# A kernel of attention and SwiGLU: the last unit's gated product taken in two parts, and seven groups of steps moved along the engine queues

## The chip, the cores and the metric

The kernel runs on one core of one Trainium2 chip. The metric is the device time of one execution in microseconds (us), as the median of several executions.

## The reference

Input `x` has 2048 rows of 576. Attention `a` has 32 heads of width 18 and four segments of 512 rows; it mixes softmax attention inside a segment with a memory `M`, `z` that earlier segments have filled. The feed-forward part `b` is a SwiGLU with an inner width of 4608. A sigmoid gate per row mixes the two.

```
g = sigmoid((x * gate_w).sum(-1))
q, k, v = x @ wq, x @ wk, x @ wv            # 32 heads of 18, segments s = 0..3 of 512 rows
per segment: p = softmax(q k^T * 18**-0.5 + mask);  a_dot = p @ v
             a_mem = phi(q) M / (phi(q) z + 1e-6);  o = sigmoid(beta) a_mem + (1 - sigmoid(beta)) a_dot
             M += phi(k)^T v;  z += sum phi(k)       # phi(t) = t + 1 if t > 0 else exp(t)
a = o @ wo
b = (silu(x @ w_gate) * (x @ w_up)) @ w_down     # 576 -> 4608 -> 576
out = g * a + (1 - g) * b
```

## The kernel before

TensorE (PE in the profile) works with operands split into a high and a low part, so that each product is made of several matmuls. The program has three stages, and each engine carries out its instructions in the order in which the code below issues them; no scheduler moves them.

**Stage 1, the segments.** The loop `for s in range(NSEG)` (L732) goes through four segments. In each come nine chains `qk(s, m, u, mid)` (n = 0 to 8, L735 to L781) of 14 matmuls (L223) into three banks in turn, for 128 columns of q or k each. ScalarE (ACT) and VectorE (DVE) split a finished chain into three bf16 parts (L455, L462, L465, and GpSimd, POOL, L466), and make phi of it (L460, L461, L468). The list `mid` holds steps of other kinds that are issued in the middle of that: `rest_sum` and `rest_split` (L651 to L658, x's last 64 rows for stage 2; tables `RSTEP` and `blocks`) in segment 2, and `first_sum` and `first_split` (L628 to L641, x for stage 2; tables `FSUM`, `FSPLIT`) in segment 3. After each chain from the second on, `next(upd)` takes one step of `upd_gen` (L496): it transposes a block of phi(k) into two banks, copies them to the tile `kt` (512 columns by ACT, L514; 64 columns by DVE, L517), and one step later multiplies it with v (L505). Then follow eight value steps `v_step` (L475: 14 matmuls L223, then ACT L484, L485, DVE L486, ACT L491, POOL L492) on the banks 5, 6 and 7 in turn, each with a memory step (`mem_step`, PE L550, DVE L553 to L557). In segment 3 these eight also issue the first steps of `w_make(0)`, which splits the first unit's weights (POOL L369, ACT L373, DVE L377, then a store): the tuple at L835 says how many per value step.

**Stage 2, the units.** Rows are taken in two halves of 1024, and the inner width in 36 tiles of 128 (f = 0 to 35): 72 units. A unit (L1510 to L1553) makes gate and up for one tile by seven products (`seven`, L1421: six matmuls L1426 and one L1429 each) into the banks `a`, `y` and `xx`, in this order: `a` 0, `y` 1, `a` 2, `xx` 3, `a` 4, `y` 5, `xx` 6. ACT copies `a` into `xx` after the first (L1519); product 2 adds into `a` and so has to wait for that copy. After 5 and 6 come the two Silu (L1540, L1542) and the two gated products on DVE (L1548 for rows 0 to 511, which needs product 6; L1549 for rows 512 to 1023, which doesn't). `split_by` has them split into `hh` (ACT L1295) and `hl` (DVE L1298). Behind each product but one stands a `tick()` (two behind 5), k = 0 to 7, which issues what `defer` put down for that beat, the down products of the last three units, and a step of attention.

The down products are 16 groups per three units, `feed(half, f)` in the order of i = 0 to 7 with two column parts each; i = 0 to 3 reads rows 0 to 511, i = 4 to 7 the others. `down_groups` (PE L1162, nine matmuls a group; the first two groups at once, so that each takes the two older tiles before the newest) adds into `ya` by DVE (L1169, L1171). Down weights are split by `d_split` (ACT L1139, DVE L1140, then L1142 or ACT L1144) under a scale from `d_look` (ACT L1116, a Square with a sum) and `d_scale` (PE L158, DVE, POOL L1128 to L1131). After unit 35 of each half the groups of the last three tiles are fed at once; in half 0 ten beats work them off (L1557), which also issue `rest_second` (POOL L1381, ACT L1388, DVE L1392), x's last rows for half 1.

`exp_table()` (L1418) has ACT load the table set for Exp ahead of its use; Silu needs another set. `gates()` (L1412) makes the row gates from an Exp.

**Stage 3** multiplies attention with `wo`, mixes and stores 16 row tiles.

Of the kernel before, what the change touches and what calls it, by code (L numbers as in the profile page):

```python
# [18 lines left out]
OP = mybir.AluOpType  # L19
# [9 lines left out]
FT = 36  # L29
# [40 lines left out]
def gated_mix(ctx, tc, xT, xrest, wf, wfr, wfh, wd, wv, wo, beta, cmask, ident, bmask, out):  # L70
# [323 lines left out]
    with ExitStack() as st:  # L394
# [101 lines left out]
        def upd_gen(s):  # L496
            acc = [pair_tile([P, 3, MW]), pair_tile([P, 2, MW])]
            Mo, Mn = Mm[s % 2], Mm[(s + 1) % 2]
            for i in range(5):
                if i:  # L500
                    for k in range(NT):
                        a, b = HR[k]
                        n = (b - a) * E
                        kk = P if k < 4 else 64
                        nc.tensor.matmul(acc[k // 3][:kk, k % 3, :n], kt[:, P * k:P * k + kk],  # L505
                                         vf[:, i - 1].rearrange("p h e -> p (h e)")[:, a * E:b * E],
                                         start=(i == 1 and k % 3 == 0), stop=(i == 4), skip_group_check=True)
                if i < 4:
                    kt = sp.tile([P, D], F32, name="kt", bufs=1)
                    c = slice(P * i, P * i + P)  # L510
                    ta = half_tile([P, 4, P])
                    for k in range(4):
                        nc.tensor.transpose(ta[:, k], phi[s, k, 1][:, c], idt)
                    nc.scalar.activation(kt[:, 0:512], ta.rearrange("p a b -> p (a b)"), AF.Copy)  # L514
                    tb = lone_tile([P, P])
                    nc.tensor.transpose(tb, phi[s, 4, 0][:, c], idt)
                    nc.vector.tensor_copy(kt[:, 512:576], tb[:, 64:128])  # L517
# [140 lines left out]
            rest_16(XR[j], rr[((0, 0), (0, 0), (1, 1), (0, 1), (1, 0), (1, 1), (0, 1))[j]])  # L658

        XR = [None] * 7  # L660
        RSTEP = {2: (0, 3), 3: (5, -1), 4: (1, -4), 5: (4, -2), 6: (2,), 7: (-6,), 8: (6,)}
        rb, rs = {}, {}

        def b_load(i):
# [56 lines left out]
        def scan_load(t):  # L721
# [7 lines left out]
        FSUM = {3: [(1, 0), (4, 0)], 4: [(2, 0), (1, 1)], 6: [(4, 1), (2, 1)], 7: [(6, 0)], 8: [(6, 1)]}  # L729
        FSPLIT = {2: [(0, 0)], 3: [(5, 0), (0, 1)], 4: [(1, 0), (4, 0)], 5: [(5, 1), (2, 0)], 6: [(1, 1), (3, 0)],  # L730
                  7: [(3, 1), (4, 1)], 8: [(2, 1)]}
        for s in range(NSEG):  # L732
            upd = upd_gen(s - 1) if s else None
            casts = []
            for n, (m, u) in enumerate(chains):  # L735
                mid = []
                if s == 0:
                    for z in loads.get(n, []):
                        z()
                    if n + 3 < 9:  # L740
                        mid.append(lambda n=n: q_split(*chains[n + 3]))
                    if n in halves:
                        mid.append(lambda n=n: v_split(*halves[n]))
                if s == 1 and n < 3:
                    cast = masks(*((0, 3), (3, NT), (0, 0))[n])
                    casts.append(cast)
                if s == 1 and 3 <= n < 6:
                    mid.append(casts[n - 3])
                if (s, n) == (1, 7):
                    mid.append(betas)  # L750
                mid += scan_step(17 * s + n)
                if (s, n) == (1, 7):
                    mid.append(lambda: total(sx, 0, 20))
                if s == 2:
                    if n == 5:
                        mid.append(lambda: weigh(1, half_tile([P, 9])))
                    if n == 0:
                        rest_load()
                    for z in blocks.get(n, ()):
                        mid.append(lambda z=z: b_step(*z))  # L760
                    for j in RSTEP.get(n, ()):
                        mid.append(lambda j=j: rest_split(j) if j >= 0 else rest_sum(-j))
                if s == 3:
                    if n < 4:
                        first_load(n)
                    for j, z in FSPLIT.get(n, []):
                        if j in (0, 3, 5):
                            mid.append(lambda j=j, z=z: first_split(j, z))
                    for j, z in FSUM.get(n, []):
                        mid.append(lambda j=j, z=z: first_sum(j, z))  # L770
                    for j, z in FSPLIT.get(n, []):
                        if j in (1, 2, 4):
                            mid.append(lambda j=j, z=z: first_split(j, z))
                if s < 3:
                    for kt in ((0, 1), (2, 3), (4,))[n - 6] if s == 0 and n > 5 else (n - 4,) if s and n > 3 else ():
                        raws["x", kt] = x_load(s + 1, kt)
                qk(s, m, u, mid)
                flush(2)
                scan_load(17 * s + n)
                if upd is not None and n > 0:  # L780
                    next(upd, None)  # L781
# [16 lines left out]
            for n in range(8):  # L798
# [23 lines left out]
                else:  # L822
                    if n == 4:
                        wraw_of[1] = [w_load(1, u) for u in range(2)]
                    if n < 2:
                        first_split(6, n)
                    for k, t, v in ((0, rhs[0][96:], 0.0), (1, kst[0], -1.0), (3, kst[1], -1.0), (4, rhs[1][96:], 0.0)):
                        if n == k:
                            nc.gpsimd.memset(t, v)
# [13 lines left out]
    with ExitStack() as st:  # L843
# [271 lines left out]
        def d_look(f):  # L1115
            nc.scalar.activation(junk, draw[f], AF.Square, accum_out=column(123 + f % CH))  # L1116
# [253 lines left out]
        def rest_second(rest):  # L1370
# [23 lines left out]
            todo = [(-1, load, 0), (0, high, 0), (0, high, 3), (1, low, 0), (1, low, 3), (4, load, 1), (11, high, 5),  # L1394
                    (11, total, 1), (12, low, 5), (12, high, 1), (13, total, 4), (13, low, 1), (14, total, 2),
                    (14, high, 4), (15, low, 4), (15, total, 6), (16, high, 2), (16, low, 2), (17, high, 6), (18, low, 6)]
            return [(o, lambda fn=fn, j=j: fn(j)) for o, fn, j in todo]

        def glance(i, k):
# [34 lines left out]
        for pos, (half, f) in enumerate(seq):  # L1434
# [49 lines left out]
            def tick():  # L1484
# [5 lines left out]
                if half == 0:  # L1490
                    g = {(0, 0): f + 2, (2, 2): f + 1, (2, 4): f + 2}.get((q, k), FT) if f > 1 else k if f == 0 and k < CH else FT
                    if g < FT:
                        draw[g] = d_load(g)
                    if (f == 2 and k < CH) or (f > 2 and q == 0 and 2 <= k < 2 + CH):
                        d_look(k if f == 2 else f + k - 2)
                    if (f, k) == (2, 3) or (f > 2 and (q, k) == (0, 5)):
                        d_scale(f // CH)
                    if (f, k) == (2, 7) or (f > 2 and (q, k) == (1, 3)):
                        d_back(f // CH)
                    if f == 2 and k > 4 or f > 2 and (q, k) in ((1, 1), (1, 7), (2, 5 + int(f < FT - 1))):  # L1500
                        g = k - 5 if f == 2 else f - 1 if k == 1 else f
# [15 lines left out]
            p5, sg0, sg1 = (row_tile() for _ in range(3))  # L1517
            seven(a, 0)
            nc.scalar.activation(xx, a, AF.Copy)  # L1519
# [20 lines left out]
            nc.scalar.activation(sg0, sg0, AF.Silu, scale=iw[f // 4])  # L1540
            seven(y, 5, False)
            nc.scalar.activation(sg1, y, AF.Silu, scale=iw[f // 4])  # L1542
# [5 lines left out]
            nc.vector.scalar_tensor_tensor(sg0, xx, hk[f // 4], sg0, op0=OP.mult, op1=OP.mult)  # L1548
            nc.vector.scalar_tensor_tensor(sg1, p5, hk[f // 4], sg1, op0=OP.mult, op1=OP.mult)  # L1549
# [116 lines left out]
```

## Time and profile before

| | |
|---|---|
| median of 3 executions | 1716.42 us (1714.65 to 1716.99) |
| the profiled execution | 1718.78 us, of which its span is 1717.1 us |
| PE busy | 1679.5 us, 98% of the span |
| DVE, ACT, POOL busy | 1353.8, 1076.6, 889.2 us |
| granted TensorE clock | 0.998 in the mean |

The span is the time from the first to the last instruction. Stage 1 ends at some 233 us of it, half 0 at 923 us, half 1 at 1631 us. In the answers of the trace, "[0.54 <-ACT bank L1519]" behind an instruction says that its engine was idle for 0.54 us before it and which instruction ended that wait; a row with "x6" merges six instructions.

### The profile page before, as it was taken

What the parts mean: (1) busy time and instruction counts of PE and PEld (TensorE: products, weight loads), DVE (VectorE), ACT (ScalarE), POOL (GpSimd) and SP (SyncE); (2) the same over time, 40 slices, a digit from 0 to 9 for tenths busy, and PEclk for the clock granted to TensorE, in tenths of its full rate; (3) what the DMA queues carried; (4) which work ended last, traced back from release to release, by engine and by line L of the source; (5) the groups of instructions that cost most, each with busy time, mean ns of one, the idle gap of its engine ahead of it and who ended that gap; (6) DMA issues with size and microseconds to landing.
All of it is one profiled execution on the core that took longest, in us unless ns stands there. A gap on an engine that the chain in (4) does not pass through costs nothing.

```text
span 1717.1 us, 35318 instructions
## 1 busy us (share of the span) xinstructions
PE 1679.5 (98%) x12269; PEld 1077.8 (63%) x12269; DVE 1353.8 (79%) x3295; ACT 1076.6 (63%) x1930; POOL 889.2 (52%) x1191
## 2 busy tenths in 40 slices
PE   9999999999999999999999999999999999999999
PEld 7898865556655665565555656556656656655577
DVE  6687676789888988898886878788878788776466
ACT  7666567777777777767774654665556566565411
POOL 3336562266667665665452665465546565554121
PEclk9999999999999999999999999999999999999999
DMA  8666675666776675446535486796696597574544
GB/s 282 218 232 222 214 260 208 208 200 177 231 223 208 168 244 192 154 121 195 169 123 164 114 192 158 163 219 136 147 215 166 121 221 167 140 163 125 156 157 145
DMA packets 349542, 314.25 MB, mean 183 GB/s; under 512 B 201268, under 2 KB 266548, under 8 KB 349364
## 3 DMA queue, kind: packets, MB, share of 16 engines
q1 hardware_dynamic: 349364, 312.00, 63.5%
q8 instruction: 96, 1.57, 0.4%
q14 instruction: 82, 0.67, 0.1%
HBM read 186.15 MB, written 99.55 MB: 166 GB/s over the span
## 4 chain that ended last, share of the span: by engine, by line
PE 73%; DVE 12%; ACT 7%; issue 3%; DMA 3%; POOL 1%; SPq 1%; DVEq 0%; ACTq 0%; POOLq 0%
PE bank L1426 31%; PE bank L1162 18%; PE bank L223 8%; PE bank L1429 5%; PE bank L889 3%; PE bank L1002 2%; DVE ya L1171 1%; PE bank L1030 1%; ACT L1540 1%; DVE junk L907 1%; PE bank L1032 1%; PE bank L964 1%; DVE p L1102 1%; ACT row L1540 1%; DMA rc<-rt 1%
## 5 line engine op out<-in xcount | busy, mean ns | idle before, releaser
L1162 PE MATMUL bank<-dw,hh 128*128 128x320 f16 (+1 forms) x2304 | 437.5, 286 | 13.3 <-DVE ya L1171 8.9
L1162 PE MATMUL bank<-dw,hl 128*128 128x320 f16 (+1 forms) x1152 | 330.1, 287 | 3.8 <-DVE hl L1298 3.2
L1106 POOL TENSOR_TENSOR p<-pe,p 128x512 f16<-128x512 f32 x220 | 271.9, 1236 | 75.3 <-DVE p L1102 50.6
L1162 PEld LDWEIGHTS <-hh 128*128 128x128 f16 x2304 | 225.3, 98 | 99.9 <-issue 18.1
L1006 ACT ACTIVATE pe<-bank 128x512 f32<-128x512 f32 x220 | 130.1, 592 | 183.6 <-PE bank L1002 167.5
L1171 DVE SCALAR_TENSOR_TENSOR ya<-bank,sc,ya 128x320 f32<-128x320 f32 x352 | 176.2, 511 | 55.0 <-PE bank L1162 53.3
L1429 PE MATMUL bank<-xr,rh 128*128 128x512 f16 x504 | 191.0, 379 | 0.0
L907 DVE CUSTOM_DVE_ANT_0 junk<-bank,cm 128x128 bf16<-128x128 f32 (+2 forms) x352 | 169.3, 481 | 13.7 <-PE bank L889 7.3
L1298 DVE SCALAR_TENSOR_TENSOR hl<-hh,row 128x512 f16<-128x512 f16 x144 | 129.7, 902 | 45.7 <-ACT hh L1295 44.8
L1014 POOL TENSOR_SCALAR_AFFINE_SELECT pe<-pe 128x256 f32<-128x256 f32 (+1 forms) x220 | 89.3, 406 | 144.9 <-ACT pe L1006 137.3
L1162 PEld LDWEIGHTS <-hl 128*128 128x128 f16 x1152 | 112.7, 98 | 34.3 <-DVE hl L1298 3.8
L889 PE MATMUL bank<-kst,qst 108*128 108x512 bf16 (+3 forms) x512 | 124.5, 299 | 3.6 <-ACT pe L1006 2.9
L1002 PE MATMUL bank<-qst,kst 111*128 111x512 bf16 (+3 forms) x352 | 103.2, 300 | 1.1 <-DVE acc L975 1.1
L1102 DVE CAST p<-pe 128x512 f16<-128x512 f32 x203 | 103.3, 510 | 0.0
L369 POOL TENSOR_TENSOR ws<-raw 128x256 f32<-128x256 f32 x72 | 65.6, 912 | 63.4 <-DMA raw<-in_wf_dram 32.2
L1538 DVE TENSOR_TENSOR row<-bank,row 128x512 f32<-128x512 f32 x72 | 49.6, 689 | 60.9 <-ACT bank L1537 60.8
L223 PE MATMUL bank<-xo,qhi 128*128 128x512 f32 x288 | 92.5, 401 | 1.3 <-ACT xo L132 0.7
L466 POOL TENSOR_TENSOR q<-qr,q 128x512 bf16<-128x512 f32 x36 | 47.8, 1329 | 84.8 <-ACT q L465 77.0
L1295 ACT ACTIVATE hh<-row 128x512 f16<-128x512 f32 x144 | 89.0, 618 | 3.7 <-DVE row L1548 3.0
L1533 ACT ACTIVATE row<-bank 128x512 f32<-128x512 f32 x72 | 42.9, 596 | 73.7 <-PE bank L1429 73.7
L1537 ACT ACTIVATE bank<-bank 128x512 f32<-128x512 f32 x72 | 41.9, 581 | 72.8 <-PE bank L1429 70.9
L1429 PEld LDWEIGHTS <-rh 128*128 128x128 f16 x504 | 49.3, 98 | 59.6 <-issue 0.2
(1102 smaller groups left out, 4213.9 us busy)
## 6 DMA issues: line engine op xcount, KB each, us to landing
xo<-in_wf_dram SPq DMA_DIRECT2D x65, 320.0 KB
raw<-in_wf_dram SPq DMA_DIRECT2D x72, 256.0 KB
dc<-dw SPq DMA_DIRECT2D x36, 432.0 KB
dw<-dc SPq DMA_DIRECT2D x36, 432.0 KB
rh<-rc SPq DMA_DIRECT2D x72, 168.0 KB
draw<-in_wd_dram SPq DMA_DIRECT2D x36, 288.0 KB
xo<-in_xT_dram SPq DMA_DIRECT2D x33, 256.0 KB
vd<-vps SPq DMA_DIRECT2D x8, 912.0 KB
```

Of the source, the lines that this page charges most:

```text
L223: nc.tensor.matmul(t, st[n], mv[n], start=(n == 0), stop=(n == 13))
L889: nc.tensor.matmul(t[:, c:c + w], qs[:KR, pr, P * i:P * i + P], ks[:KR, pr, 0:w], start=True, stop=True)
L907: nc.vector.tensor_tensor_reduce(junk.bitcast(BF)[:, :w], t[:, c:c + w], cm[:, L - w:L], 1.0, -3.0e38, OP.add, OP.max, m[:, k:k + 1])
L1002: nc.tensor.matmul(t[:, c:c + w], ks[:KR + 3, pr, P * j:P * j + P], qs[:KR + 3, pr, P * j:L], start=True, stop=True)
L1006: nc.scalar.activation(pe, t, AF.Exp, scale=SCALE)
L1102: nc.vector.tensor_copy(p1, pe)
L1106: nc.gpsimd.tensor_sub(p2, pe, p1)
L1162: nc.tensor.matmul(t, p, d[:, q, cs], start=(f == CH * c and n == 0), stop=(f == CH * c + CH - 1 and n == 2))
L1171: nc.vector.scalar_tensor_tensor(ya[:, i, cs], t, inv[c], ya[:, i, cs], op0=OP.mult, op1=OP.add)
L1298: nc.vector.scalar_tensor_tensor(lo, hi, -STEP, src, op0=OP.mult, op1=OP.add)
L1426: nc.tensor.matmul(t, w[:, p, z], x[z][:, q], start=first and n == 0, stop=False, skip_group_check=True)
L1429: nc.tensor.matmul(t, rem[:, RPOS[j]], XR[j], start=False, stop=True, skip_group_check=True)
```

## The change

Eight edits, all of order; no product is added or left out.

1. `kt`: its last 64 columns are copied by ACT instead of DVE.
2. Segment 2: `rest_sum(6)` goes from chain 7 to chain 6, and `rest_split(6)` from the middle of chain 8 to behind it.
3. Segment 3: `first_sum(6, 1)` and `first_split(2, 1)` go from chain 8 to the value steps 1 and 0; `first_split(6, z)` from value steps 0 and 1 to 2 and 3.
4. The first weights' steps are issued about one value step earlier.
5. `rest_second`: its second part two beats later.
6. The three first `d_look` go from unit 2 to unit 1, `d_scale` from beat 3 of unit 2 to beat 1; the last `d_split` of half 0 from beat 5 of unit 35 to beat 2.
7. No Exp table in unit 0 and at the start of unit 3; `gates()` at the end of unit 3.
8. In unit 35 the gated product of rows 512 to 1023 comes ahead of product 6, those rows are split first, and the 16 groups start with i = 4 to 7.

```diff
-                    nc.vector.tensor_copy(kt[:, 512:576], tb[:, 64:128])
+                    nc.scalar.activation(kt[:, 512:576], tb[:, 64:128], AF.Copy)
...
-        RSTEP = {2: (0, 3), 3: (5, -1), 4: (1, -4), 5: (4, -2), 6: (2,), 7: (-6,), 8: (6,)}
+        RSTEP = {2: (0, 3), 3: (5, -1), 4: (1, -4), 5: (4, -2), 6: (2, -6)}
...
                 qk(s, m, u, mid)
+                if (s, n) == (2, 8):
+                    rest_split(6)
...
-                    if n < 2:
-                        first_split(6, n)
+                    if n == 0:
+                        first_split(2, 1)
+                    if n == 1:
+                        first_sum(6, 1)
+                    if 2 <= n < 4:
+                        first_split(6, n - 2)
...
-                    for _ in range((0, 0, 2, 1, 2, 2, 2, 2)[n]):
+                    for _ in range((0, 1, 2, 2, 2, 2, 2, 2)[n]):
...
         def feed(half, f):
-            return [(f // CH, i, hf, hs, ds, half) for i in range(8) for hf in range(2)]
+            return [(f // CH, i, hf, hs, ds, half) for i in ((4, 5, 6, 7, 0, 1, 2, 3) if f == FT - 1 else range(8))
+                    for hf in range(2)]
...
-                    if (f == 2 and k < CH) or (f > 2 and q == 0 and 2 <= k < 2 + CH):
-                        d_look(k if f == 2 else f + k - 2)
-                    if (f, k) == (2, 3) or (f > 2 and (q, k) == (0, 5)):
+                    if (f == 1 and 4 <= k < 4 + CH) or (f > 2 and q == 0 and 2 <= k < 2 + CH):
+                        d_look(k - 4 if f == 1 else f + k - 2)
+                    if (f, k) == (2, 1) or (f > 2 and (q, k) == (0, 5)):
                         d_scale(f // CH)
...
-                    if f == 2 and k > 4 or f > 2 and (q, k) in ((1, 1), (1, 7), (2, 5 + int(f < FT - 1))):
+                    if f == 2 and k > 4 or f > 2 and (q, k) in ((1, 1), (1, 7), (2, 6 if f < FT - 1 else 2)):
...
-            if half == 0 and q == 0 and f:
+            if half == 0 and q == 0 and f > CH:
                 exp_table()
-                if f == CH:
-                    gates()
...
-            if (half or q == 0) and not cps:
+            if (half or q == 0 and f) and not cps:
                 exp_table()
+                if half == 0 and f == CH:
+                    gates()
             tick()
             tick()
+            gated = [lambda: nc.vector.scalar_tensor_tensor(sg0, xx, hk[f // 4], sg0, op0=OP.mult, op1=OP.mult),
+                     lambda: nc.vector.scalar_tensor_tensor(sg1, p5, hk[f // 4], sg1, op0=OP.mult, op1=OP.mult)]
+            parts, first = [(hh[:, z], hl[:, z], (sg0, sg1)[z]) for z in range(2)], int(f == FT - 1)
+            if first:
+                gated[1]()
             seven(xx, 6, False)
-            nc.vector.scalar_tensor_tensor(sg0, xx, hk[f // 4], sg0, op0=OP.mult, op1=OP.mult)
-            nc.vector.scalar_tensor_tensor(sg1, p5, hk[f // 4], sg1, op0=OP.mult, op1=OP.mult)
-            split_by(2, hh[:, 0], hl[:, 0], sg0, int(q < CH - 1))
-            split_by(3, hh[:, 1], hl[:, 1], sg1)
+            gated[0]()
+            if not first:
+                gated[1]()
+            split_by(2, *parts[first], int(q < CH - 1))
+            split_by(3, *parts[1 - first])
```

The tables `FSUM` and `FSPLIT` lose their entries of chain 8, and the second part of `rest_second`'s list has every beat raised by two.

**Place one**, DVE at the end of half 0 (unit 35): before, from the sum that follows product 4 (L1538) to the first addition into `ya`. L1140 and L1142 split the last down weight, L1355 belongs to half 1's x.

```order
L1538 TENSOR_TENSOR row<-bank_11775,row 128x512
L1355 SCALAR_TENSOR_TENSOR xo_10317<-xr_10334,sc,xo_10317 128x512
L1140 SCALAR_TENSOR_TENSOR dw<-draw,sc,dw 128x576
L1548 SCALAR_TENSOR_TENSOR row<-bank_11842,sc,row 128x512
L1549 SCALAR_TENSOR_TENSOR row<-row,sc 128x512
L1142 TENSOR_SCALAR dw<-dw 128x576
L1298 SCALAR_TENSOR_TENSOR hl<-hh,row 128x512 x2
```

The same place with the change; L1146 and L1148 are the down weight, L1543 the sum, L1555 and L1554 the gated products, L1304 `hl`.

```order
L1146 SCALAR_TENSOR_TENSOR dw<-draw,sc,dw 128x576
L1543 TENSOR_TENSOR row<-bank_11773,row 128x512
L1148 TENSOR_SCALAR dw<-dw 128x576
L1362 SCALAR_TENSOR_TENSOR xo_10315<-xr_10332,sc,xo_10315 128x512
L1555 SCALAR_TENSOR_TENSOR row<-row,sc 128x512
L1554 SCALAR_TENSOR_TENSOR row<-bank_11843,sc,row 128x512
L1304 SCALAR_TENSOR_TENSOR hl<-hh,row 128x512 x2
```

The down weight now stands ahead of the sum, and the gated product without a bank ahead of the one with a bank.

**Place two**, ACT from the fourth product of unit 1 to unit 2's copy of `a` (L1519): before.

```order
L1537 ACTIVATE bank_2952<-bank_2887 128x512
L373 ACTIVATE wo__2956<-ws,sc 128x512
L1540 ACT_TABLE_LOAD
L1540 ACTIVATE row<-row,sc 128x512
L1542 ACTIVATE row<-bank_2925,sc 128x512
L373 ACTIVATE wo__2985<-ws,sc 128x512
L1519 ACTIVATE bank_2991<-bank_2989 128x512
```

With the change (L1542 is now the copy after product 4, L1122 is `d_look`, L1526 the copy of `a`).

```order
L1542 ACTIVATE bank_2951<-bank_2886 128x512
L1122 ACTIVATE junk,sc<-draw 128x576
L373 ACTIVATE wo__2956<-ws,sc 128x512
L1545 ACTIVATE row<-row,sc 128x512
L1547 ACTIVATE row<-bank_2924,sc 128x512
L1122 ACTIVATE junk,sc<-draw 128x576 x2
L373 ACTIVATE wo__2987<-ws,sc 128x512
L1526 ACTIVATE bank_2993<-bank_2991 128x512
```

A table load has gone and three Squares have come, ahead of the copy of `a`.

**Place three**, ACT in segment 3 from value step 2 to value step 4: before.

```order
L484 ACTIVATE vf<-bank_2523 128x16x18
L485 ACTIVATE vps_131<-bank_2523 128x16x18
L491 ACTIVATE vps_131<-r_2538 128x16x18
L484 ACTIVATE vf<-bank_2557 128x16x18
L485 ACTIVATE vps_131<-bank_2557 128x16x18
L491 ACTIVATE vps_131<-r_2572 128x16x18
L373 ACTIVATE wo__2590<-raw,sc 128x512
L484 ACTIVATE vf<-bank_2594 128x16x18
```

With the change.

```order
L484 ACTIVATE vf<-bank_2520 128x16x18
L485 ACTIVATE vps_131<-bank_2520 128x16x18
L491 ACTIVATE vps_131<-r_2535 128x16x18
L136 ACTIVATE xo_2551<-ph_2179,sc 128x512
L373 ACTIVATE wo__2555<-raw,sc 128x512
L484 ACTIVATE vf<-bank_2557 128x16x18
L485 ACTIVATE vps_131<-bank_2557 128x16x18
L491 ACTIVATE vps_131<-r_2572 128x16x18
L136 ACTIVATE xo_2551<-ph_2181,sc 128x512
L373 ACTIVATE wo__2592<-ws,sc 128x512
L484 ACTIVATE vf<-bank_2598 128x16x18
```

Three more instructions of ACT (two L136, one L373) stand ahead of value step 4's first copy.

More of the change, by code (lines that the diff above doesn't have):

```diff
@@ L728, in gated_mix @@
         blocks = {3: [(0, 0)], 4: [(0, 1)], 5: [(0, 2), (1, 0)], 6: [(1, 1)], 7: [(1, 2)]}
-        FSUM = {3: [(1, 0), (4, 0)], 4: [(2, 0), (1, 1)], 6: [(4, 1), (2, 1)], 7: [(6, 0)], 8: [(6, 1)]}
+        FSUM = {3: [(1, 0), (4, 0)], 4: [(2, 0), (1, 1)], 6: [(4, 1), (2, 1)], 7: [(6, 0)]}
         FSPLIT = {2: [(0, 0)], 3: [(5, 0), (0, 1)], 4: [(1, 0), (4, 0)], 5: [(5, 1), (2, 0)], 6: [(1, 1), (3, 0)],
-                  7: [(3, 1), (4, 1)], 8: [(2, 1)]}
+                  7: [(3, 1), (4, 1)]}
         for s in range(NSEG):
@@ L1392, in low @@
                 nc.vector.scalar_tensor_tensor(t, source(j)[32:64], sx[32:64], t, op0=OP.mult, op1=OP.subtract)
-            todo = [(-1, load, 0), (0, high, 0), (0, high, 3), (1, low, 0), (1, low, 3), (4, load, 1), (11, high, 5),
-                    (11, total, 1), (12, low, 5), (12, high, 1), (13, total, 4), (13, low, 1), (14, total, 2),
-                    (14, high, 4), (15, low, 4), (15, total, 6), (16, high, 2), (16, low, 2), (17, high, 6), (18, low, 6)]
+            todo = [(-1, load, 0), (0, high, 0), (0, high, 3), (1, low, 0), (1, low, 3), (4, load, 1), (13, high, 5),
+                    (13, total, 1), (14, low, 5), (14, high, 1), (15, total, 4), (15, low, 1), (16, total, 2),
+                    (16, high, 4), (17, low, 4), (17, total, 6), (18, high, 2), (18, low, 2), (19, high, 6), (20, low, 6)]
             return [(o, lambda fn=fn, j=j: fn(j)) for o, fn, j in todo]
@@ L1499, in tick @@
                         d_back(f // CH)
-                    if f == 2 and k > 4 or f > 2 and (q, k) in ((1, 1), (1, 7), (2, 5 + int(f < FT - 1))):
-                        g = k - 5 if f == 2 else f - 1 if k == 1 else f
+                    if f == 2 and k > 4 or f > 2 and (q, k) in ((1, 1), (1, 7), (2, 6 if f < FT - 1 else 2)):
+                        g = k - 5 if f == 2 else f - 1 if (q, k) == (1, 1) else f
                         ds[half, g] = d_split(g, draw.pop(g))
```

## The prediction

> **What bounds the kernel now.** I read the page first, for the busy shares.
>
> ```profile
> span 1717.1 us, 35318 instructions
> PE 1679.5 (98%) x12269; PEld 1077.8 (63%) x12269; DVE 1353.8 (79%) x3295; ACT 1076.6 (63%) x1930; POOL 889.2 (52%) x1191
> ```
>
> PE is idle for 1717.1 − 1679.5 = 37.6 us, and no matmul is added or removed. So the change can win only idle time of PE, or time in which PE runs at a lower clock. The second view is therefore the list of PE's waits by what ended them (us in total, times, longest).
>
> ```profile
> PE bank L1162 <- DVE ya L1171: 8.9, 18, 1.0
> ...
> PE bank L505 <- DVE kt L517: 1.8, 2, 1.1
> PE bank L1426 <- ACT bank L1519: 1.7, 3, 0.6
> ...
> PE bank L550 <- DVE ph L468: 1.3, 1, 1.3
> ...
> PE bank L1162 <- DVE dw L1140: 1.1, 1, 1.1
> ```
>
> The largest entry belongs to the steady down products, which the change leaves in their order. All others are single places at the ends of stages, where the edits sit. The third view is the table of windows (length; busy PE, PEld, DVE, ACT, POOL with counts; PE clock; DMA share; GB/s), laid over those places.
>
> ```profile
> 156.80:160.20 3.40, 2.05 (x16) 1.82 (x15) 3.34 (x7) 2.00 (x5) 1.16 (x1) 1.00 0.06 5
> 273.60:277.00 3.40, 1.45 (x10) 0.64 (x8) 2.77 (x6) 2.66 (x7) 0.00 (x0) 1.00 0.89 319
> 277.00:280.40 3.40, 3.40 (x13) 1.70 (x12) 2.54 (x7) 1.21 (x3) 1.45 (x2) 0.50 1.03 392
> 901.65:905.06 3.41, 1.34 (x12) 0.90 (x11) 3.41 (x6) 2.47 (x4) 1.43 (x1) 1.00 0.27 101
> 905.00:908.50 3.50, 3.50 (x17) 2.29 (x16) 1.08 (x3) 0.00 (x0) 0.00 (x0) 0.51 0.97 290
> ```
>
> In two windows PE is busy for less than 1.5 of 3.4 us, and each time the clock granted in the following 3.4 us is 0.50. After the window with 2.05 busy I see no such fall. So a stall of some 2 us at the wrong phase costs PE another 3.4 × 0.5 = 1.7 us.
>
> **Part by part.** The sum is made against the profiled execution, 1718.78 us (span 1717.1 and 1.7 around it), 2.4 above the median of the runs shown. All gains are in us of PE time.
>
> *1. The key copies.* `kt`'s last 64 columns wait on DVE behind other work.
>
> ```profile
> 65.50 0.21 DVE L517 COPY kt<-bank 128x64 f32<-128x64 f32 x1
> ...
> 192.27 0.58 ACT L514 ACTIVATE kt<-bank 128x512 f32<-128x512 f32 x1
> 194.74 0.60 ACT L455 ACTIVATE q<-bank 128x512 bf16<-128x512 f32 x1 [1.90 <-issue]
> 196.41 0.35 PE L505 MATMUL bank<-vf,kt 128*64 128x76 f32 x2 [0.72 <-DVE kt L517]
> 202.88 0.60 ACT L455 ACTIVATE q<-bank 128x512 bf16<-128x512 f32 x1 [4.16 <-DMA stw<-q]
> ```
>
> The two waits are 1.1 and 0.72, together 1.8. On ACT the copy stands right behind its 512-column half, where ACT is idle for 1.90 at 192.85. The trace has no ACT copy of 64 columns. It lies between 0.19 (one column, the row at 259.44 below) and 0.58 (512 columns). I take 0.25, nearer the small one, twelve times, under ACT's idle time. Where that cover is gone each copy delays ACT's next split by 0.25. Gain 1.5, from 1.1 to 1.8: the second wait lies ahead of a chain that waits on a transfer (4.16 at 202.88), and part of it may be swallowed there.
>
> *2. Segment 2's remainder.*
>
> ```profile
> 154.25 1.28 POOL L654 TENSOR_TENSOR xo<-xo,xo 128x512 f32<-128x512 f32 x1
> 154.31 2.77 DVE L137 SCALAR_TENSOR_TENSOR xr<-xr,sc,xr 128x384 f16<-128x384 f32 x1
> ...
> 159.07 0.69 DVE L468 SCALAR_TENSOR_TENSOR ph<-bank,ph 128x512 f32<-128x512 f32 x1
> ```
>
> L468 frees the bank for which the memory step's L550 waits 1.3. `rest_split(6)`, whose DVE part stands ahead of L468, goes behind it, and POOL's L654 moves a chain earlier, away from the slow L137. Gain 1.3; the lower bound is 0.7, one DVE operation as long as L468 still in front.
>
> [...]
>
> *3. Value steps, units 0 to 3.* ACT's queue changes most here.
>
> ```profile
> 220.81 0.70 ACT L136 ACTIVATE xo<-ph,sc 128x512 f16<-128x512 f32 x1
> 245.88 1.28 ACT L1419 ACT_TABLE_LOAD   x1
> 248.53 1.46 PE L1426 MATMUL bank<-xo,wo__2849 128*128 128x512 f16 x6 [0.53 <-ACT bank L1519]
> 252.95 0.72 POOL L369 TENSOR_TENSOR ws<-raw 128x256 f32<-128x256 f32 x1 [6.56 <-DMA raw<-in_wf_dram]
> 258.87 0.67 ACT L1116 ACTIVATE junk<-draw 128x576 f16<-128x576 f32 x1
> 259.44 0.19 ACT L1116 ACTIVATION_READ_ACCUMULATOR junk<-draw 128x1 f32 x1
> 262.94 0.38 PE L158 MATMUL bank<-sc 128*128 128x3 f32 x2 [0.35 <-ACT junk L1116]
> ```
>
> Now PE loses 1.7 in three waits for the copy of `a` (units 0, 1 and 3; 0.53 of it in unit 1), 0.35 for the scale, and 3.40 − 1.45 = 1.95 in the window at 273.60, chiefly for the first down weights: 4.0 in all. I replayed ACT's queue in its new order with these durations:
> - Value step 4 gets three more instructions in front (3 × 0.70 = 2.1); about half of that is idle now, so the steps and unit 0's copy come some 0.5 late, and that wait grows from 0.54 to 1.06.
> - Unit 1 loses the Exp table load (1.28): its 0.53 goes.
> - Unit 2 gets three Squares (3 × 0.86 = 2.6) for one table load, ahead of its copy of `a`; the split between them waits for weights that landed at 252.95. A new wait of 0.65.
> - The scale is made two beats earlier: 0.35 goes.
> - Unit 3 loses a table load and `gates()` at its start: 0.64 goes to 0.3, and the first down weights come 1.3 to 1.7 earlier: 1.95 to 0.75.
>
> What is left is 1.06 + 0.65 + 0.3 + 0.75 = 2.76: gain 4.0 − 2.76 = 1.25, taken as 1.3. The bounds are 4.0 (all gone) and −1.0 (ACT 2.1 late instead of 1.06 through the value steps, and again in unit 2).
>
> *4. The half clock at 277.* With at most 1 us idle in that window it goes: 1.7, or 0.
>
> *5. `gates()`* puts two small DVE operations (at most 0.21 each, as L517) into the end of unit 3: −0.2; none if DVE is idle there.
>
> *6. The end of half 0.*
>
> ```profile
> 889.29 0.73 DVE L1549 SCALAR_TENSOR_TENSOR row<-row,sc 128x512 f32<-128x512 f32 x1
> ...
> 897.83 0.67 ACT L1542 ACTIVATE row<-bank,sc 128x512 f32<-128x512 f32 x1
> ...
> 898.87 0.43 PE L1162 MATMUL bank<-dw,hh 128*128 128x320 f16 x2
> ...
> 900.14 2.94 POOL L1381 TENSOR_TENSOR raw<-raw 128x512 f32<-128x512 f32 x2 [14.30 <-DVE dw L1140]
> 900.59 1.36 DVE L1549 SCALAR_TENSOR_TENSOR row<-row,sc 128x512 f32<-128x512 f32 x1
> 900.71 0.63 ACT L1295 ACTIVATE hh<-row 128x512 f16<-128x512 f32 x1 [1.55 <-DVE row L1548]
> 901.39 0.45 PE L1162 MATMUL bank<-dw,hh 128*128 128x320 f16 x2 [0.89 <-ACT hh L1295]
> ...
> 903.17 1.28 DVE L1298 SCALAR_TENSOR_TENSOR hl<-hh,row 128x512 f16<-128x512 f16 x2
> 903.90 0.31 PE L1162 MATMUL bank<-dw,hl 128*128 128x320 f16 x1 [2.06 <-DVE hl L1298]
> ```
>
> PE wants `hh` at 901.39 − 0.89 = 900.50 and waits 0.89 + 2.06 = 2.95 here. With the down weight split ahead of it, the gated product of rows 512 on needs only the Silu that ended at 898.50: it runs to about 899.3, and `hh` of those rows to 899.9, in time. The product with the bank follows to about 900.0 (product 6 was done by 898.87), then `hl` in 0.64 to 900.65. PE needs it some 0.1 after it needed `hh`. If POOL's L1381, which starts when its data land at 900.0, slows `hl` as it seems to have slowed L1549 (1.36 instead of 0.73), 0.65 is left. Gain 2.5, from 2.3 to 2.95. Late next would be the second half's `hl`, needed five groups later, so covered.
>
> *7. The half clock at 905.* The cause, 2 us idle in 3.4, is gone: 1.7, or 0.
>
> [...]
>
> *8. The end of half 1.*
>
> ```profile
> 1632.87 2.42 DVE L1298 SCALAR_TENSOR_TENSOR hl<-hh,row 128x512 f16<-128x512 f16 x2
> ...
> 1634.70 0.31 PE L1162 MATMUL bank<-dw,hl 128*128 128x320 f16 x1 [1.10 <-DVE hl L1298]
> ```
>
> The same reordering brings `hl` forward by about one gated product (0.73), but two `hl` take 2.42 here instead of 1.28. Gain 0.6, from 0 to 1.1.
>
> Edit 5's later beats cost nothing as long as x's last rows are ready before unit 0 of half 1; the ten beats after unit 35 hide them, and without that cover it is a beat or two of PE.
>
> The sum: 1.5 + 1.3 + 1.3 + 1.7 − 0.2 + 2.5 + 1.7 + 0.6 = 10.4. From 1718.78 that makes 1708.4 for a profiled execution, and against the median 1716.4 − 10.4 = **1706.0 us**. All terms at their bounds give 14.5 and 2.9.
>
> **The rivals.**
> - *The half clock stays* because shorter stalls remain in the same windows, or because it falls for other reasons: terms 4 and 7 are nothing, 1706.0 + 3.4 = 1709.4. For it: where the windows begin against the stalls is not in my hand. Against it: 2.05 busy left the clock at 1.00, and I expect over 2.4.
> - *ACT becomes the bound between 213 and 277*: term 3 is −1.0 and term 4 nothing, 1706.0 + 2.3 + 1.7 = 1710.0. For it: three Squares and two L136 now stand ahead of instructions for which PE waits. Against it: four table loads of 1.28 go.
> - *The front's gains are swallowed*: segment 3 waits for transfers (4.16 at 202.88), so what is won ahead of it comes to nothing. Terms 1 and 2 are gone, 1708.8. Against it: the first wait and bank 2's lie in segments 0 and 2.
> - *Slower:* the shifted phase of units against attention and DMA makes the down products wait longer for `ya`. Now that is 8.9 in 18 waits, in 24 groups of three units. If each waited the longest, 1.0, it would be 24 − 8.9 = 15.1 more: 1721.1. It decides from 10.4 / 24 = 0.43 us a group on. For it: the wait is there already and varies from none to 1.0. Against it: the order inside these units is the old one.
>
> **How the numbers follow.** A measurement of this kernel tells some 0.2%, 3.4 us, from no change. Chances: the forecast 0.50; the half clock stays 0.13; ACT the bound 0.14; the front swallowed 0.08; the longer `ya` waits 0.15, of which 0.08 end within 0.2% and 0.07 beyond it. All but the last are faster by more than 3.4 us: 0.85, 0.08, 0.07. The range takes in the first four: 1701.5 (nearly all terms at their upper bounds) to 1711.5 (ACT's case and 1.5 of the front's loss).
>
> **What would show it.** Right: no wait L505 <- `kt`, no L550 <- `ph` in segment 2; PE's clock 1.00 after the ends of unit 2 and of half 0; at the end of half 0 at most 0.65 of waiting; a new wait for the copy of `a` in unit 2. Wrong: PE's waits between 213 and 277 sum to more than 4.8, the clock at half in the same places, or the waits L1162 <- `ya` well above 8.9.

## The result, and the profile after

The changed kernel takes 1710.42 us in the median of 6 runs (1709.46 to 1711.85), before takes 1717.48 on the same chip (1714.65 to 1719.42): 7.06 us less, a ratio of 0.9958 with a 95% interval of 0.9946 to 0.997. The forecast was 1706.0 (10.4 less), with a range of 1701.5 to 1711.5. The direction was right and the time lies inside the range, but a third of the forecast gain is missing, and the experiments below put it in one place, the first units of stage 2.

The page of the changed kernel, for the same two rows as before:

```profile
span 1707.9 us, 35311 instructions
PE 1677.2 (98%) x12269; PEld 1078.1 (63%) x12269; DVE 1351.4 (79%) x3283; ACT 1073.0 (63%) x1936; POOL 889.1 (52%) x1191
```

PE's idle time went from 37.6 to 1707.9 − 1677.2 = 30.7 us, and its busy time fell by 2.3, of which some 1.7 is one half-clock stretch fewer (3.41 us at a clock of 0.50; before has two while PE works, the changed kernel one). The profiled executions differ by 9.2 in span, 2.1 more than the medians. Of these, 1.3 are at the program's start, which the change does not touch: in the list of waits of before, PE waits there for the first splits of x, and in this execution of the changed kernel neither row exists.

```profile
PE bank L223 <- ACT xo L132: 0.7, 2, 0.5
PE bank L223 <- DVE xo L133: 0.6, 2, 0.4
```

PE's waits after the change, by what ended them (us in total, times, longest):

```profile
PE bank L1168 <- DVE ya L1177: 7.1, 17, 0.9
PE bank L1168 <- DVE ya L1175: 4.6, 3, 2.7
...
PE bank L1433 <- ACT bank L1526: 2.5, 3, 2.0
...
PE bank L1168 <- DVE dw L1148: 0.6, 1, 0.6
...
PE bank L1168 <- DVE hl L1304: 0.2, 1, 0.2
```

The waits for `kt` by DVE and for `ph` are gone, the steady waits for `ya` (L1177, the old L1171) went from 8.9 to 7.1, and `hl` from 3.2 to 0.2. Two entries have grown: the copy of `a` (L1526, the old L1519) from 1.7 to 2.5, with one wait of 2.0, and the first additions into `ya` (L1175, the old L1169) from 1.9 to 4.6, with one wait of 2.7 that did not exist.

The end of half 0 in the timeline after (start, length, engine, line):

```profile
895.54 0.75 DVE L1555 SCALAR_TENSOR_TENSOR row<-row,sc 128x512 f32<-128x512 f32 x1 [0.24 <-ACT row L1547]
...
896.21 0.75 DVE L1554 SCALAR_TENSOR_TENSOR row<-bank,sc,row 128x512 f32<-128x512 f32 x1
...
896.33 1.29 ACT L1301 ACTIVATE hh<-row 128x512 f16<-128x512 f32 x2 [0.82 <-DVE row L1555]
...
896.99 2.37 DVE L1304 SCALAR_TENSOR_TENSOR hl<-hh,row 128x512 f16<-128x512 f16 x2
...
897.43 3.06 POOL L1388 TENSOR_TENSOR raw<-raw 128x512 f32<-128x512 f32 x2 [14.85 <-DMA raw<-in_xr_dram]
...
897.74 0.31 PE L1168 MATMUL bank<-dw,hl 128*128 128x320 f16 x1 [0.23 <-DVE hl L1304]
```

The product without a bank now runs first, `hh` is in time (no wait for it is left), and of 2.95 us of waiting 0.23 remains. The two `hl` take 2.37 with POOL's L1388 beside them instead of 1.28, but the long one is the second (0.69 and 1.70), which PE needs only groups later.

The start of stage 2 went the other way. Unit 0's copy of `a`, and PE's wait for it:

```profile
234.48 0.59 ACT L1526 ACTIVATE bank<-bank 128x512 f32<-128x512 f32 x1
...
235.12 1.42 PE L1433 MATMUL bank<-xo,wo__2592 128*128 128x512 f16 x4 [2.04 <-ACT bank L1526]
```

And unit 3, nearly 50 us later, in time order:

```profile
282.14 0.74 ACT L140 ACTIVATE xo<-xo 128x640 f32<-128x640 f32 x1 [2.30 <-DMA xo<-in_wf_dram]
...
282.88 0.58 ACT L1542 ACTIVATE bank<-bank 128x512 f32<-128x512 f32 x1
...
283.49 0.69 DVE L1543 TENSOR_TENSOR row<-bank,row 128x512 f32<-128x512 f32 x1 [3.13 <-ACT bank L1542]
...
284.10 0.54 DVE L1175 TENSOR_SCALAR ya<-bank,sc 128x320 f32<-128x320 f32 x1
...
284.69 0.43 PE L1168 MATMUL bank<-dw,hh 128*128 128x320 f16 x2 [2.66 <-DVE ya L1175]
```

Read it upwards: PE waits for the addition L1175, which stands on DVE behind the sum L1543, which waits for ACT's copy L1542, which stands on ACT behind L140, a Square with a sum over weights of later units that a transfer (L1412) has only just brought. Three engines in a row wait for one DMA. (Some expectations below call this place unit 4, and L1412's weights x; unit 4's own copy of `a` comes only at 303.33.)

### The profile page after: what moved, and what is told of

It reads as the page before. It is cut to its first block, busy times and chain, and to the rows that moved or that the text cites. A ratio compares the mean times of both kernels' runs of the same rounds, so it can differ in the third digit from the quotient of the medians.

```text
span 1707.9 us, 35311 instructions
## 1 busy us (share of the span) xinstructions
PE 1677.2 (98%) x12269; PEld 1078.1 (63%) x12269; DVE 1351.4 (79%) x3283; ACT 1073.0 (63%) x1936; POOL 889.1 (52%) x1191
## 4 chain that ended last, share of the span: by engine, by line
PE 77%; DVE 10%; ACT 7%; DMA 2%; issue 2%; POOL 1%; SPq 1%; DVEq 0%; ACTq 0%; POOLq 0%
PE bank L1433 32%; PE bank L1168 18%; PE bank L223 10%; PE bank L1436 5%; PE bank L895 3%; PE bank L1008 2%; PE bank L1036 1%; DVE ya L1177 1%; ACT L1545 1%; DVE junk L913 1%; PE bank L505 1%; PE bank L1038 1%; DMA xo<-in_wf_dram 1%; PE bank L970 1%; DVE p L1108 1%
## 5 line engine op out<-in xcount | busy, mean ns | idle before, releaser
L1177 DVE SCALAR_TENSOR_TENSOR ya<-bank,sc,ya 128x320 f32<-128x320 f32 x352 | 176.2, 511 | 52.2 <-PE bank L1168 50.7
L1304 DVE SCALAR_TENSOR_TENSOR hl<-hh,row 128x512 f16<-128x512 f16 x144 | 133.0, 924 | 42.5 <-ACT hh L1301 41.6
L1543 DVE TENSOR_TENSOR row<-bank,row 128x512 f32<-128x512 f32 x72 | 49.6, 689 | 62.4 <-ACT bank L1542 62.3
L1538 ACT ACTIVATE row<-bank 128x512 f32<-128x512 f32 x72 | 42.9, 596 | 75.7 <-PE bank L1436 75.6
L1542 ACT ACTIVATE bank<-bank 128x512 f32<-128x512 f32 x72 | 41.9, 581 | 71.1 <-PE bank L1436 69.2
```

The lines of the kernel that those rows point to most:

```text
L1177: nc.vector.scalar_tensor_tensor(ya[:, i, cs], t, inv[c], ya[:, i, cs], op0=OP.mult, op1=OP.add)
L1304: nc.vector.scalar_tensor_tensor(lo, hi, -STEP, src, op0=OP.mult, op1=OP.add)
```

## The experiments

The experiments ran in three groups of four, with before beside each group (1717.83, 1718.39 and 1718.37 us in the median). My theory after seeing the two traces, A, was that the change's parts add up, that the ends and the front win and that the middle loses, mostly through ACT's longer queue ahead of unit 0. The rival is that transfers pace the units from 3 on.

**1. The ends of the halves alone.** Before with edits 5 and 8 and the last down weight's beat.

```diff
-                    if f == 2 and k > 4 or f > 2 and (q, k) in ((1, 1), (1, 7), (2, 5 + int(f < FT - 1))):
+                    if f == 2 and k > 4 or f > 2 and (q, k) in ((1, 1), (1, 7), (2, 6 if f < FT - 1 else 2)):
...
+            if first:
+                gated[1]()
             seven(xx, 6, False)
```

> Before with edits 5, 8 and the last down weight of edit 6 alone (the ends of the halves). Theory A, the parts add up: the waits at the end of half 0 fall from 2.96 to some 0.2, the half clock there (1.7) goes, and the 1.1 at the end of half 1 goes: 5.5 us faster than before. Rival, the half clock does not hang on that stall: 3.8 us faster, with the clock at 0.50 still shown near 905.

Measured: 1712.50 us, ratio 0.997 (0.9958 to 0.9981), 5.3 less than before, where theory A had 5.5. The interval, 3.3 to 7.2 less, takes in the rival's 3.8 too. In the profile the waits at the end of half 0 are down to 0.23 and the clock near 905 is 1.00; at the end of half 1, 0.58 of the 1.1 is left.

**2. The front alone.** Before with edits 1 and 2.

```diff
-                    nc.vector.tensor_copy(kt[:, 512:576], tb[:, 64:128])
+                    nc.scalar.activation(kt[:, 512:576], tb[:, 64:128], AF.Copy)
...
+                if (s, n) == (2, 8):
+                    rest_split(6)
```

> Before with edits 1 and 2 alone (the key copies and segment 2's remainder). Theory A: the waits for kt (1.8) and for phi in segment 2 (1.35 and 0.27) go and 0.5 of a new wait comes in segment 2: 2.9 us faster than before. Rival, segment 3's chain over transfers swallows it: 0 to 1 us faster, with longer waits of PE between 200 and 240.

Measured: 1715.06 us, ratio 0.9982 (0.9973 to 0.9991), 2.8 less, with an interval of 1.5 to 4.6. That is more than the rival's 0 to 1, so segment 3's transfers do not swallow it.

**3. The middle alone.** Before with edits 3, 4, 7 and the first scales of edit 6.

```diff
-                    for _ in range((0, 0, 2, 1, 2, 2, 2, 2)[n]):
+                    for _ in range((0, 1, 2, 2, 2, 2, 2, 2)[n]):
...
-                    if (f, k) == (2, 3) or (f > 2 and (q, k) == (0, 5)):
+                    if (f, k) == (2, 1) or (f > 2 and (q, k) == (0, 5)):
```

> Before with edits 3, 4, the first scales of edit 6, and edit 7 (value steps, units 0 to 4). Theory A: this part loses time, since unit 0's copy comes 1.5 later than PE wants it, which also brings a half clock of 1.7 us, and unit 4 waits 2.7 for its first additions: 1 to 2.5 us slower than before. The rival is the forecast's own sum for these terms: 2.8 us faster.

Measured: 1718.20 us, ratio 1.0 (0.999 to 1.0009). It neither wins nor loses, so the forecast's 2.8 are not there; the loss that theory A expected isn't shown either. In its profile the two new waits are there, 1.76 at unit 0's copy and 1.89 at unit 3's additions, but no half clock behind unit 0 (its profile has 0.999 in the mean, which the one fall at 900.89 makes up). The three parts sum to −5.3 − 2.8 + 0.4 = −7.7, against 7.1 and, in the second group (experiment 5), 8.0 for the whole change.

**4. The change without edits 3 and 4.** It tells whether ACT's longer queue in the value steps is what spoils the middle. Edit 3's lines are shown with experiment 9.

```diff
-                    for _ in range((0, 1, 2, 2, 2, 2, 2, 2)[n]):
+                    for _ in range((0, 0, 2, 1, 2, 2, 2, 2)[n]):
```

> The change without edits 3 and 4 (value steps and first weights as before). Theory A: the wait for unit 0's copy falls from 2.0 to some 0.5 and the half clock at 236 goes: 3 us faster than the change, 10 faster than before. Rival, transfers pace units 3 and 4: what is won ahead is lost again in a longer wait at 282, and the time is the change's own, 7 us faster than before.

Measured: 1711.71 us, ratio 0.9956 (0.9943 to 0.997), the change's own time. Its waits of PE between 225 and 300:

```profile
PE bank L1164 <- DVE ya L1171: 3.7, 3, 1.6
PE bank L1429 <- ACT bank L1522: 1.5, 3, 0.7
```

The copy of `a` costs 1.5 instead of 2.5, with no wait over 0.7, and yet nothing is won in the median. The wait for `ya` is still 3.7 in this stretch, as with the change: 1.05 and 1.60 stand in place of the 2.66, with 1.03 behind them where the change has 1.04. Theory A fell on the size: edits 3 and 4 cost little. The rival's reason isn't shown either, since the wait for `ya` did not grow. What both kernels have is that wait.

**5. The changed kernel again**, unaltered, beside the next three.

> The changed kernel unaltered, to be compared with the next three on one chip. Every theory: 1710.4 us, 7 us faster than before.

Measured: 1710.38 us, ratio 0.9958 (0.9945 to 0.997).

**6. The down weights' loads later.** SP (SyncE) issues the transfers, one after the other (0.33 to 0.99 us each between 269 and 275 in the changed kernel). The one for which L140 waits was issued late, at 274.17. Its waits between 250 and 290 in the changed kernel have this on top:

```profile
SPq L317 <- DVE dw L1146: 11.4, 2, 10.7
```

The load of down weight 3 (L317) is issued at beat 2 of unit 2 and needs a buffer that DVE's split frees at beat 5. For 10.7 us, from 256.5 to 267.2, nothing behind it on SP is issued. The experiment issues it, and the next one, later:

```diff
-                    g = {(0, 0): f + 2, (2, 2): f + 1, (2, 4): f + 2}.get((q, k), FT) if f > 1 else k if f == 0 and k < CH else FT
+                    g = {(0, 0): f + 2, (2, 2 if f > 2 else 6): f + 1, (2, 4 if f > 2 else 7): f + 2}.get((q, k), FT) if f > 1 else k if f == 0 and k < CH else FT
```

> The changed kernel with the loads of down weights 3 and 4 moved from beats 2 and 4 of unit 2 to its beats 6 and 7. Theory T, unit 4 is paced by a burst of transfers: SP stands at the first of these loads for 10.7 us (256.5 to 267.2) until the buffer is free, so x's loads (L1412) land late, ACT's sum L140 stands ahead of the copy L1542, and PE waits 2.7 for ya at 282. With the loads later, SP passes earlier, the DMA engines work between 257 and 268, and that wait goes: 2 to 2.7 us faster than the change. Rival, the additions are late because of DVE's and ACT's own queue (gates, sums): the wait stays at 2.7 and the time is the change's.

Measured: 1707.28 us, ratio 0.9939 (0.9927 to 0.9952), 3.1 less than the change beside it; the runs of the two (1705.13 to 1708.61, and 1707.91 to 1712.18) hardly overlap. The windows of the stretch in which SP stood and of the one after it, first the change (length; busy PE, PEld, DVE, ACT, POOL; clock; DMA share; GB/s):

```profile
256.50:267.20 10.70, 10.41 (x51) 4.89 (x50) 7.74 (x14) 8.98 (x18) 5.06 (x7) 1.00 0.13 40
272.00:282.00 10.00, 9.41 (x64) 6.15 (x63) 4.92 (x11) 3.97 (x10) 1.67 (x2) 1.00 1.03 372
```

Then with the later loads:

```profile
256.50:267.20 10.70, 10.70 (x53) 5.01 (x52) 7.86 (x14) 8.87 (x16) 7.11 (x9) 1.00 0.42 131
272.00:282.00 10.00, 10.00 (x70) 6.63 (x69) 5.86 (x14) 6.36 (x15) 0.00 (x0) 1.00 1.00 360
```

The DMA engines, nearly empty before the burst (0.13), now carry 0.42 there, and PE has no gap in either window. ACT's copy in unit 3 is late no more: what it waits for now is PE itself.

```profile
278.17 0.58 ACT L1542 ACTIVATE bank<-bank 128x512 f32<-128x512 f32 x1 [0.55 <-PE bank L1436]
```

And of PE's waits between 225 and 300 in this kernel the 2.7 is gone:

```profile
PE bank L1433 <- ACT bank L1526: 2.2, 2, 2.0
PE bank L1168 <- DVE ya L1175: 1.0, 1, 1.0
```

The first three loads of L1412 were issued at 270.69, 271.69 and 274.17 with the change, and at 261.51, 266.92 and 271.33 here. SP still stands at L317, but for 6.2 in all and 4.0 at most.

Theory T holds: the wait of 2.7 hung on SP's blocked queue. Without it the kernel is 11.1 under before (8.2 to 12.5), which takes in the forecast's 10.4. The kernel before did not run with the later loads.

**7. The later loads, without edits 3 and 4.** The diffs are those of 4 and 6.

> The same later loads, without edits 3 and 4. Theory T: as the later loads alone, and unit 0's wait 0.7 instead of 2.0, with unit 2's at 0.9 instead of 0.3: 2.5 to 4.5 us faster than the change. Rival, edits 3 and 4 shift the wait only from one unit to another: the same time as the later loads alone.

Measured: 1706.66 us, ratio 0.9939 (0.9926 to 0.9953): the same as 6. Unit 0's wait is 0.7, and unit 2 waits 0.9 and 0.7 instead. In the profiles, edits 3 and 4 shift a wait from one unit to another.

**8. The change without edit 7 and the first scales of edit 6.**

```diff
-                    if (f == 1 and 4 <= k < 4 + CH) or (f > 2 and q == 0 and 2 <= k < 2 + CH):
+                    if (f == 2 and k < CH) or (f > 2 and q == 0 and 2 <= k < 2 + CH):
...
-            if half == 0 and q == 0 and f > CH:
+            if half == 0 and q == 0 and f:
                 exp_table()
```

> The change without the first scales of edit 6 and without edit 7 (tables and gates in their old places, edits 3 and 4 kept). If edits 6 and 7 are worth what the forecast gave them: 0.53, 0.35, 0.3 and 1.2 of waits and, more often than not, a half clock come back, and the 2.7 at 282 goes: 1 us slower than the change. If the wait at 282 takes all they win: the change's own time within 0.5 us.

Measured: 1712.68 us, ratio 0.9968 (0.9957 to 0.9979), 2.3 slower than the change beside it; in its profile the waits of 0.53, 0.35, 0.64 and 1.95 are back, and the 2.7 at 282 is 0.2. So these edits are worth some 2 us here, more than either theory had. That they would be worth more if the wait in unit 3 did not take a part is argued from the 2.7 that shrinks to 0.2, not shown.

**9. The later loads, edit 3 undone.**

```diff
-                    if n == 0:
-                        first_split(2, 1)
-                    if n == 1:
-                        first_sum(6, 1)
-                    if 2 <= n < 4:
-                        first_split(6, n - 2)
+                    if n < 2:
+                        first_split(6, n)
```

> The change with the later loads of down weights, and edit 3 undone (edit 4 kept). If the 2.0 at unit 0 comes from edit 3's splits of x on ACT's queue: that wait falls to some 0.7 with no new wait in unit 2, 1.3 us faster than the later loads alone (about 1706). If it comes from edit 4's earlier weights: the wait stays at 2.0 and the time is that of the later loads alone (1707.3).

Measured: 1706.40 us, ratio 0.9929 (0.9915 to 0.9944). Its waits of PE between 225 and 300:

```profile
PE bank L1429 <- ACT bank L1522: 1.7, 3, 0.9
PE bank L1164 <- DVE ya L1171: 1.4, 2, 1.0
```

Unit 0's wait falls from 2.0 to 0.9, so it comes from edit 3's splits on ACT's queue; 0.7 in unit 2 and 0.4 in unit 3 come back for it. The 0.9 us between 6 and 9 are less than their runs scatter.

**10. The later loads, edit 4 undone.** The diff is the line shown with experiment 4.

> The change with the later loads, and edit 4 undone (edit 3 kept). If the 2.0 at unit 0 comes from edit 4's earlier weight split: it falls to some 1.3, and unit 2 waits 0.9 and 0.7 as without both edits, so 1 us slower than the later loads alone. If it comes from edit 3: 2.0 stays and unit 2's waits come on top, 1.6 us slower.

Measured: 1707.42 us, ratio 0.9938 (0.9923 to 0.9953), the time of 6. Unit 0's wait for the copy is 0.7, but now PE waits 0.4 and 0.5 inside unit 0 for the weights themselves (L377). Both theories missed that: the weights come later, PE arrives later, and the copy looks earlier.

**11. The ends without the early down weight.** As 1, with the split left at beat 5.

> Before with edits 5 and 8, the last down weight left at beat 5. If the early split of the down weight is needed for the gain (it stands on DVE ahead of the gated product of rows 512 on): PE waits some 1.5 to 2 at the end of half 0, and 2.5 to 3.5 us faster than before. If edit 8 alone does it: 5.3 us faster, as with the split moved.

Measured: 1714.07 us, ratio 0.9975 (0.9965 to 0.9985), 4.3 less than before. Its end of half 0:

```profile
898.90 0.82 DVE L1140 SCALAR_TENSOR_TENSOR dw<-draw,sc,dw 128x576 f16<-128x576 f32 x1 [1.10 <-ACT dw L1139]
899.63 0.75 DVE L1549 SCALAR_TENSOR_TENSOR row<-row,sc 128x512 f32<-128x512 f32 x1
...
901.10 0.45 PE L1162 MATMUL bank<-dw,hh 128*128 128x320 f16 x2 [0.90 <-ACT hh L1295]
...
902.33 0.31 PE L1162 MATMUL bank<-dw,hl 128*128 128x320 f16 x1 [0.79 <-DVE hl L1298]
```

L1549 needs nothing but stands behind the down weight's split, as expected: 0.90 and 0.79 are left of the waits, where 1 leaves 0.23. The waits are those of the first theory (1.7 in all), but the time lies between the two theories: in the median the early split is worth 1 us or so, less than the intervals tell.

**12. The ends without edit 5.**

> Before with edit 8 and the early last down weight, without edit 5 (x's last rows at their old beats). If POOL's and ACT's work on x's rows stands beside the last splits, edit 5 is worth 0.5 to 1.5 us, and this is 4 to 5 us faster than before; if edit 5 does nothing, 5.3 us faster.

Measured: 1713.52 us, ratio 0.9977 (0.9967 to 0.9986), 4.9 less than before, against 5.3 with edit 5 in another group. The wait at the end of half 0 is 0.24 here and 0.23 there. What edit 5 is worth stays open; it isn't what removes the stall.

## Why the prediction was right, and where not

- **Terms 1 and 2** (2.8): measured alone, 2.8. The key copies take 0.21 each on ACT (0.25 was assumed), and PE's waits for `kt` by ACT stay at 0.3. The waits that went come to more than the terms (1.8 and 1.6), but a new wait of 0.6 in segment 2, for the value step's L486, takes some of it.
- **Terms 6, 7 and 8** (2.5 + 1.7 + 0.6 = 4.8): measured alone, 5.3, with an interval (3.3 to 7.2) too wide to tell one term from another. In the profile, 2.95 came down to 0.23, at the upper part of its bounds: of the two `hl` beside POOL's step only the second is long (0.69 and 1.70), which PE needs late. The 1.1 at the end of half 1 went whole in the changed kernel's profile and to about half in that of experiment 1. One reading was off without harm: by the rows at 901.39 and 903.90, PE needs `hl` 0.45 after `hh`, not 0.1.
- **Terms 3, 4 and 5** (1.3 + 1.7 − 0.2 = 2.8): measured alone, 0.4 slower, with an interval of 1.7 faster to 1.5 slower (0.999 to 1.0009 of 1718). This is the step that failed. The waits that were to go went: 0.53, 0.35 and all but 0.6 of the 1.95. Unit 0's copy was put 0.5 late and came 1.5 late, so that wait is 2.04 instead of 1.06. But the replay put the others too high, and the four waits that it left come to 2.04 + 0.29 + 0.16 + 0.59 = 3.08 in the changed kernel, against 2.76 in the sum. What is missing is a wait that stands nowhere in the sum, the 2.66 in unit 3. The replay followed ACT's queue and took the transfers as given. In before, SP passed its blocked load at 269.36, and PE came to this place at 287.25 and did not wait. With the change, PE was there at 282.03, 5.2 earlier, but SP passed only 2.1 earlier, at 267.25. The row for it was in the trace of before, in SP's own waits between 250 and 290, which I had not read as a bound:

```profile
SPq L317 <- DVE dw L1140: 13.3, 3, 11.6
```

  (`gates()`, term 5, issues three small DVE operations, not two; no run shows it alone.)
- **The signs** came out as named: no wait for `kt` by DVE, none for `ph`, 0.23 at the end of half 0, 0.29 for the copy of `a` in unit 2, and 3.9 us of waits between 213 and 277, under the 4.8 that would have been wrong. But the wait that the sum lacks lies at 282, behind the stretch that they watched.
- **The half clock** (terms 4 and 7) was taken by the sum as fixed to its stall; only a rival said that its phase isn't in hand. In these profiles it isn't fixed, as the last section shows: the changed kernel's lost the two at 277.00 and 905.06 and got one back at 235.61, behind unit 0's wait.
- **The rivals.** "ACT becomes the bound" names the right stretch, but its price (4.0) was put on ACT alone, and undoing ACT's steps won nothing in the median. That its time, 1710.0, is nearly the one measured is luck: it comes from taking away term 4 and 2.3 of term 3, and the runs show another cause. "The front's gains are swallowed" fell with experiment 2. The longer `ya` waits of the steady units did not come: 8.9 became 7.1.

The best of the kernels that ran are those with the later loads: 1707.28, 1706.66, 1706.40 and 1707.42 us, not told apart, and some 11 us (0.6 to 0.7%) under before.

## What to carry to other kernels

Before a gain is booked, look at what the engine will meet when it arrives earlier. Here PE came to the first down products 5.2 us earlier, but SP passed the load that waited for its buffer only 2.1 us earlier. That load stood in SP's order long before its buffer was free, and for 10.7 us nothing behind it was issued. Moving two such loads down by four and three beats was worth 3.1 us, about as much as the front edits together. So read the waits of the transfer queues as well as those of the engines, even where nobody waits for them yet.

## What the hardware showed

Stalls of like length did not cost the same clock here. In before the clock falls to 0.50 at 277.00 and at 905.06, each time for 3.413 us, and the two lie 184.0 times that apart; in the changed kernel, 235.61 and the last fall, at the program's end at 1706.76, lie 431.0 times that apart. The longest single waits of PE in the 3.41 us ahead of the falls at 277.00, 905.06 and 235.61 are 1.14, 2.06 and 2.04. The windows below have the length of such a fall and are laid in steps of it from a fall of the same execution. Laid so, experiment 2 shows the whole stall at the end of half 0, the same 2.95 us as in before, and no fall behind it:

```profile
896.00:899.41 3.41, 2.06 (x15) 1.18 (x13) 3.10 (x4) 1.22 (x3) 2.08 (x2) 1.00 0.19 70
899.41:902.82 3.41, 1.80 (x14) 1.39 (x15) 3.01 (x5) 2.16 (x4) 0.78 (x1) 1.00 0.49 144
902.82:906.23 3.41, 3.41 (x31) 2.80 (x29) 2.46 (x5) 0.00 (x0) 0.93 (x1) 1.00 0.99 313
```

The stall lies across two windows, and PE (first figure behind the length) is busy for 1.8 or more in each. Experiment 3 has one window with 1.52 us of busy PE and one with 0.89, here with the stretch that follows each; the clock is 1.00 behind the first and 0.50 behind the second:

```profile
283.08:286.49 3.41, 1.52 (x13) 1.08 (x12) 1.35 (x4) 2.66 (x7) 0.00 (x0) 1.00 1.04 408
286.49:289.90 3.41, 3.41 (x24) 2.23 (x23) 2.38 (x10) 1.66 (x4) 0.00 (x0) 1.00 0.99 367
897.48:900.89 3.41, 0.89 (x7) 0.26 (x4) 3.41 (x4) 2.06 (x4) 2.86 (x2) 1.00 0.01 3
900.89:904.30 3.41, 2.93 (x12) 1.79 (x13) 2.00 (x4) 1.03 (x2) 0.00 (x0) 0.50 0.79 261
```

In the changed kernel, unit 0's wait fell whole into one window, with the clock at 0.50 behind it, and the 2.66 of unit 3 across two (2.05 and 2.12 of busy PE), with 1.00 behind both:

```profile
232.20:235.61 3.41, 1.37 (x8) 0.54 (x6) 2.58 (x10) 2.83 (x8) 1.61 (x3) 1.00 0.80 267
235.61:239.02 3.41, 3.41 (x10) 1.19 (x9) 1.40 (x3) 0.36 (x1) 2.81 (x4) 0.50 0.74 282
...
279.98:283.40 3.42, 2.05 (x17) 1.46 (x15) 0.38 (x1) 1.26 (x4) 0.00 (x0) 1.00 1.05 382
```

In the second execution of that kernel (experiment 5) it was the other way round, with waits of 2.0 and 2.4; behind the first window, from 234.83 to 238.24, the clock is 1.00:

```profile
231.42:234.83 3.41, 1.51 (x7) 0.59 (x6) 2.55 (x12) 2.54 (x7) 1.07 (x2) 1.00 0.88 304
...
279.21:282.62 3.41, 1.12 (x10) 0.85 (x9) 1.09 (x3) 2.44 (x6) 0.00 (x0) 1.00 1.04 380
282.62:286.03 3.41, 3.30 (x13) 1.82 (x13) 1.76 (x7) 1.51 (x4) 0.00 (x0) 0.50 0.90 337
```

In the kernel with the later loads (experiment 6), the same stall of 2.0 at unit 0 leaves 1.49 of busy PE in its window, and the clock behind it is 1.00:

```profile
233.78:237.19 3.41, 1.49 (x7) 0.68 (x7) 2.18 (x7) 2.20 (x6) 1.81 (x3) 1.00 0.81 289
237.19:240.60 3.41, 3.41 (x17) 1.57 (x16) 1.27 (x2) 1.31 (x3) 2.06 (x3) 1.00 0.77 306
```

Laid so from 10 us on, to 1714 us in before and to the fall at 1706.76 in the changed kernel, the two profiles have the clock at 0.50 behind four windows, those with 1.34 to 1.46 us of busy PE, and at 1.00 behind all others, where PE is busy for 2.05 or more. In the windows of the experiments above it is 0.50 behind 0.89 and 1.12, and 1.00 behind 1.49, 1.51, 1.52, 1.80 and 2.06. What sets the clock is not shown. The changed kernel's stall of 2 us at unit 0 was followed by a half clock in one execution (some 1.7 us more, half of 3.41) and by none in the other; that this is part of why one kernel's runs scatter by several us is argued, not shown.
